# A convolution and an MLP on one core: W_out and block 2's x move to GpSimd's DMA ring, the tap diagonals move to VectorE

## The chip, the cores and the metric

The kernel runs on one core of one Trainium2 chip. The metric is the device time of one execution in microseconds. It was measured in 13 runs before the change: median 686.0, lowest 682.02, highest 687.27. The profile is that of a single execution. It has its own time (685.98) and a span from the first to the last instruction (684.2), which is 1.74 us shorter.

The engines are called as in the profile: PE is TensorE (PEld its weight loads), DVE is VectorE, ACT is ScalarE, POOL is GpSimd, SP is SyncE. SP and ACT issue DMAs into hardware queues (q1 and q10 in the profile), POOL into a software queue (q0).

## What is computed

The input x has 8 sequences of 4096 tokens and 192 channels. Each channel is filtered by a causal convolution of 7 taps, whose weights are a softmax over the taps, one set for each group of 24 channels. Then follows an MLP on 32768 tokens: 192 to 2048 channels, exact gelu, 2048 back to 192.

```python
w = np.exp(w - max); w = w / (sum + 1e-9)                 # weight: 8 heads x 7 taps
out[b, s, h, g] = sum_k w[h, k] * x_pad[b, s + k, h, g]   # 6 zeros ahead of each sequence
h = x @ w_in                                              # 192 -> 2048
g = 0.5 * h * (1 + erf(h / sqrt(2)))
y = g @ w_out                                             # 2048 -> 192, f32
```

Inputs and output are f32.

## The kernel before

**Tiling.** The tokens are split in two halves of 16384, which stand on partitions 0 to 63 and 64 to 127; 192 channels make three column pieces p of 64. The halves are cut into blocks n: six of 256 tokens per half, then blocks of 512 (`WS`). For each block the first product (`mm1`, line 740) runs in units: 8 of them for a block of 256 tokens, each with 12 matmuls and two 128-wide pieces of the 2048 channels. One gelu on ACT (line 652, 128x1024) empties a unit. PE alternates between two PSUM tiles for it (`hp`), so unit u waits for the gelu of unit u - 2. The second product of block n - 1 (`mm2`, line 771, for the small blocks, `mm2_t`, line 801, later) is spread behind the units of block n: 128 matmuls behind 8 units. The list `share` says how many come behind which unit of block 1; without an entry every unit gets the same, 16 matmuls.

**Convolution.** For blocks 0 and 1 (`PC`) PE does it with diagonal matrices: `dg` holds 7 diagonals of 64x64, made from the identity `idb` and the softmax weights `wcol` (line 397, on POOL). Each tap is a pair of matmuls (`pconv`, line 682). The bf16 copy of x that they read comes from transposes of `xin` on DVE (`trans`, line 508), then a cast by ACT for block 0 (line 225) and by POOL for block 1 (line 227). The sums leave PSUM by ACT and DVE (`conv_out`, lines 200 and 202). Block 0's taps come first of all; block 1's stand behind block 0's units 3, 4 and 5 (`behind`). From block 2 on DVE convolves: one transpose, then a first tap (line 529, or ACT's line 625 for blocks 4 to 6) and six more (line 536), and `mm1` of the block waits for the last.

**Loads.** Every DMA is issued in the order in which its engine's program stands. SP: the small weight, half of block 0's x, then a wait until W_in's second part has landed (`S_WIN[1]`), three chunks of W_out in f32 (line 853), block 2's x, the fourth chunk, block 3's x, and from there block n + 3 and the stores of block n - 1 in turn. ACT: the other half of block 0's x. POOL: two DMAs of W_in (f32 in HBM, bf16 in SBUF: the transfer casts; line 376), two of block 1's x, the diagonals when the softmax is ready, two more of block 1's x, W_in's second pair, a wait for the diagonals, `halo(1)` (the 6 tokens ahead of block 1, line 421), the three casts of block 1, `halo(2)`, and then for each chunk of W_out a wait for its landing and a cast to bf16 (line 431), which PE's second product waits for (`S_WOG`, line 838). W_in is loaded for one half of the channels on each partition half; DVE copies it across (`dup`, line 472).

**Warm-up.** PE starts with 10 matmuls of 512 columns on a zeroed tile (`warm`, line 666), behind DVE's memset of that tile.

Of the kernel before, what the change touches and what calls it, by code (L numbers as in the profile page):

```python
# [5 lines left out]
ALU = mybir.AluOpType  # L6
# [5 lines left out]
def bass_lightweight_conv__then__act_gelu_exact_kernel(  # L12
# [83 lines left out]
    def sbt(name, shape, dt):  # L96
        return es.enter_context(nc.sbuf_tensor(name, shape, dt))
# [4 lines left out]
    def sem(name):  # L102
        return es.enter_context(nc.semaphore(name))

    def ap(t, off, pat):
        return bass.AP(t, off, pat)

    with es:
# [7 lines left out]
        wnt = sbt("wnt", [32, 32], F32)  # L116
        wex = sbt("wex", [H, KS], F32)
        wcol = sbt("wcol", [128, 32], F32)
        woutf = sbt("woutf", [128, NF * C], F32)
        idb = sbt("idb", [128, 64], BF16)  # L120
        dg = sbt("dg", [128, KS * 64], BF16)
        warm = sbt("warm", [128, 512], BF16)
        hot = sbt("hot", [1, 2], F32)
        xTb = [sbt("xTb%d" % i, [128, NP * XB], BF16) for i in range(len(PC))]
        xin = [sbt("xin%d" % i, [128, TB // 32 * DQ], F32) for i in range(NX)]
# [8 lines left out]
        S_WSB = sem("S_WSB")  # L134
        S_WIN = [sem("S_WIN%d" % i) for i in range(3)]
        S_WOUT = [sem("S_WOUT%d" % i) for i in range(4)]
        S_WOG = sem("S_WOG")
        S_XIN = [sem("S_XIN%d" % i) for i in range(NX)]
        S_XP = sem("S_XP")
        S_OUT = [sem("S_OUT%d" % i) for i in range(2)]  # L140
        S_MSET = sem("S_MSET")
        S_IDN = sem("S_IDN")
        S_WARM = sem("S_WARM")
        S_PRO = sem("S_PRO")
        S_ACTP = sem("S_ACTP")
        S_DG = sem("S_DG")
# [73 lines left out]
        def cast(e, n, p):  # L220
            e.wait_ge(S_TR, NP * n + p + 1)
            dst = ap(xTb[PC[n]], p * XB + HX, [[NP * XB, 128], [1, WS[n]]])
            src = ap(xT[n % 2], p * XW + HX, [[NP * XW, 128], [1, WS[n]]])
            if n == 0:
                ins = e.activation(out=dst, in_=src, func=AF.Copy)  # L225
            else:
                ins = e.tensor_copy(dst, src)
            ins.then_inc(S_CAST[PC[n]])
# [13 lines left out]

        def xin_at(n):

            return 64 * (n // NX + (n % NX != 1))

        def banks(m, g):

# [123 lines left out]
        @block.gpsimd  # L372
        def _(g):
            def win_in(c0, c1, sm):
                for hf in range(2):
                    g.dma_start(
                        ap(win, 64 * hf * NP * F + c0, [[NP * F, 64], [F, NP], [1, c1 - c0]]),
                        ap(wint, hf * FH + c0, [[NP * F, 64], [F, NP], [1, c1 - c0]]),
                    ).then_inc(sm[hf], 16)
# [13 lines left out]
            win_in(FP[0], FP[1], [S_WIN[0]] * 2)  # L393
            load(g, 1, (0, 2), S_XP)
            g.wait_ge(S_PRO, 9)
            g.wait_ge(S_IDN, 2)
            g.tensor_tensor(  # L397
                ap(dg, 0, [[KS * 64, 128], [64, KS], [1, 64]]),
                ap(idb, 0, [[64, 128], [0, KS], [1, 64]]),
                ap(wcol, 0, [[32, 128], [1, KS], [0, 64]]),  # L400
                ALU.mult,
            ).then_inc(S_DG)
            load(g, 1, (1, 3), S_XP)
            win_in(FP[1], FP[2], S_WIN[1:])

            g.wait_ge(S_DG, 1)

            def halo(n):

                t, tw = (xTb[PC[n]], XB) if n in PC else (xT[n % 2], XW)  # L410
                dst = ap(t, HF, [[NP * tw, 128], [tw, NP], [1, HB]])
                if n >= 4:
                    g.wait_ge(S_CV, cvd(n - 2))
                if OFF[n] % SEQ == 0:
# [6 lines left out]
                g.tensor_copy(dst, src).then_inc(S_HALO)  # L421

            g.wait_ge(S_IDN, 2)
            halo(1)
            for p in range(NP):
                cast(g, 1, p)
            halo(2)
            for k in range(4):
                g.wait_ge(S_WOUT[k], 16)
                pat = [[NF * C, 128], [8 * C, 2], [1, 2 * C]]  # L430
                g.tensor_copy(ap(wout, 2 * k * C, pat), ap(woutf, 2 * k * C, pat)).then_inc(S_WOG)  # L431
            for n in range(3, NB):
                halo(n)

        @block.vector
        def _(v):
            v.memset(warm[:, :], 0.0).then_inc(S_WARM)  # L437
            v.memset(idb[:, :], 1.0).then_inc(S_MSET)
            v.memset(wnm[:, :], 0.0).then_inc(S_MSET)
            v.memset(ap(xTb[0], HF, [[NP * XB, 128], [XB, NP], [1, HB]]), 0.0).then_inc(S_HALO)  # L440
# [44 lines left out]
            def trans(n, p):  # L485

                w = WS[n]
                if p == 0:
                    v.wait_ge(S_XP if n == 1 else S_XIN[n % NX], 64 if n == 1 else xin_at(n))
                    if n >= 2 and n - 2 in PC:  # L490
                        wait_pc(v, n - 2, NP - 1)
                    elif n >= 2:
                        v.wait_ge(S_CV, cvd(n - 2))
                    if n >= 2:
                        v.wait_ge(S_HALO, n)
                if n in PC:
# [11 lines left out]
                v.transpose(out, src).then_inc(S_TR)  # L508
# [45 lines left out]
                else:  # L554
                    conv(*op[1:])

            for p in range(NP):
                trans(0, p)
            for j in PV:
                conv_out(v, 0, j)  # L560
# [100 lines left out]

        @block.tensor
        def _(t):
            t.wait_ge(S_WARM, 1)
            for i in range(10):
                t.matmul(hp[1][:, 0:512], warm[:, 0:128], warm[:, :])  # L666

            def pconv(n, kd, k):

# [26 lines left out]
            for kd in [0] * 4 + [1, 0] * 3 + [1, 2, 2] * 3 + [1, 2] + [3] * 7:  # L696
                pconv(*seq[kd].pop(0))

            behind = {
                (0, 3): [(1, kd, k) for k in taps if k > 3 for kd in (0, 1)],  # L700
                (0, 4): [(1, kd, k) for k in taps if k <= 3 for kd in (0, 1)],
                (0, 5): [(1, kd, k) for k in taps for kd in (2, 3)],
            }

            def mm1(n, i):
                w, c = WS[n], NCH[n]
# [73 lines left out]
                    ins.then_inc(S_MM2 if ph == 1 else S_PH)  # L780


            share = {1: [4, 4, 4, 10, 10, 10, 11, 11]}

            def mm2_t(m, ps, i):

# [39 lines left out]
            for n in range(NB):  # L826
                todo = units(n - 1) if n >= 1 else []
                for i in range(NSL[n]):
                    mm1(n, i)
                    for q in behind.get((n, i), []):  # L830
                        pconv(*q)
                    new = M0 < n <= M1
                    ws = SHARE if new else share.get(n, [1] * NSL[n])
                    a0 = len(todo) * sum(ws[:i]) // sum(ws)
                    a1 = len(todo) * sum(ws[: i + 1]) // sum(ws)
                    for un in todo[a0:a1]:
                        if n == 1 and un[:2] == (0, 0) and un[2] % 4 == 0:
                            t.wait_ge(S_WOG, 1 + un[2] // 4)
                        (mm2_t if new else mm2)(n - 1, *un)
            m = NB - 1  # L840
            for g2 in range(0, NG[m], 2):
# [5 lines left out]
        @block.sync  # L847
        def _(sp):
            sp.dma_start(wsb[:, :], ap(wt, 0, [[KS, H], [1, KS]])).then_inc(S_WSB, 16)
            load(sp, 0, (0, 1))  # L850

            def wout_in(k):
                sp.dma_start(  # L853
                    ap(woutf, 2 * k * C, [[NF * C, 128], [8 * C, 2], [1, 2 * C]]),
                    ap(woutt, 256 * k * C, [[2 * C, 128], [1024 * C, 2], [1, 2 * C]]),
                ).then_inc(S_WOUT[k], 16)

            sp.wait_ge(S_WIN[1], 16)
            for k in range(3):
                wout_in(k)  # L860
            load(sp, 2)
            wout_in(3)
            load(sp, 3)
            for n in range(1, NB):
                if n + 3 < NB:
                    load(sp, n + 3)
                store(sp, n - 1)
            for g in range(NG[NB - 1]):
# [31 lines left out]
```

## Time and profile before

| what | value |
|---|---|
| median of 13 runs | 686.0 us (682.02 to 687.27) |
| profiled execution | 685.98 us, span 684.2 us, mean granted clock 0.998 |
| PE busy | 676.3 us, 99% of the span |
| ACT, DVE, POOL busy | 536.5, 528.2, 31.9 us (78%, 77%, 5%) |
| chain that ended last | 96% PE, 2% DMA, 1% SP's queue |
| W_out's chunks, issue by SP | 11.19 to 12.8 (three), 15.38 (the fourth) |
| POOL's casts of the chunks begin | 14.68, 16.80, 18.99, 22.47 us |

A line of the timeline has the start in us, the length of the group in us, engine, line of the kernel, operation, output and inputs, shape and count; in square brackets is how long the engine stood idle before it and what ended that. The chain is the work that ended last, followed back from the end. A row of stretches gives the length, the busy time of PE, PEld, DVE, ACT and POOL with the number of instructions in brackets, the granted clock of PE (1.00 is full), the share of the DMA engines and GB/s.

### The profile page before, as it was taken

The numbers are of one execution on the slowest core, as the hardware profiler recorded it, in microseconds if no ns is written. First come the engines' busy times: TensorE is split into PE (matmuls) and PEld (weight loads), VectorE is DVE, ScalarE is ACT, GpSimd is POOL, SyncE is SP. The second block draws the span as 40 slices with busy tenths as digits, with TensorE's granted clock in tenths as the row PEclk, the third lists the DMA queues.
The fourth block names the chain that finished last, engine by engine and source line by source line (L and its number), as shares of the span: only waits on it lengthen the run. The fifth ranks groups of instructions, "written<-read, shape, count | busy, mean of one in ns | idle before, by whom it ended". The sixth has DMA issues, their size and how long they took to land.

```text
span 684.2 us, 26995 instructions
## 1 busy us (share of the span) xinstructions
PE 676.3 (99%) x12570; PEld 409.0 (60%) x12570; DVE 528.2 (77%) x610; ACT 536.5 (78%) x547; POOL 31.9 (5%) x56
## 2 busy tenths in 40 slices
PE   8899999999999999999999999999999999999998
PEld 5799755555555555555555555555555555555557
DVE  6779989777798777798777897777897777987511
ACT  7699987777787877778777778777877777877772
POOL 5100000000000000000000000000000000000000
PEclk9999999999999999999999999999999999999999
DMA  7544421244432244422334322334322434220123
GB/s 167 102 117 106 95 71 48 50 94 95 94 84 45 62 94 95 94 71 44 77 94 95 93 58 47 87 94 95 90 50 52 95 94 94 71 54 21 48 49 94
DMA packets 132480, 54.43 MB, mean 80 GB/s; under 512 B 126352, under 2 KB 132304, under 8 KB 132368
## 3 DMA queue, kind: packets, MB, share of 16 engines
q1 hardware_dynamic: 130224, 50.94, 31.8%
q8 instruction: 98, 1.61, 1.1%
q0 software_dynamic: 1024, 1.18, 1.0%
q10 hardware_dynamic: 1120, 0.59, 0.3%
q14 instruction: 14, 0.11, 0.1%
HBM read 28.31 MB, written 25.17 MB: 78 GB/s over the span
## 4 chain that ended last, share of the span: by engine, by line
PE 96%; DMA 2%; SPq 1%; POOL 0%; DVE 0%; issue 0%; ACT 0%; ACTq 0%
PE hp L740 47%; PE ob L801 42%; PE ob L771 6%; DMA woutf<-in_moe_w_out_dram 1%; PE hp L771 1%; DMA win<-in_moe_w_in_dram 1%; SPq L853 0%; SPq L339 0%; DMA wsb<-in_weight_dram 0%; POOL xin L339 0%; POOL wout L431 0%; POOL dg L397 0%; DVE wcol L460 0%; ACT wex L593 0%; DVE osb L295 0%
## 5 line engine op out<-in xcount | busy, mean ns | idle before, releaser
L652 ACT ACTIVATE gT<-hp 128x1024 bf16<-128x1024 f32 x512 | 523.1, 1024 | 133.3 <-PE hp L740 130.0
L740 PE MATMUL hp<-xc,win 64*64 64x512 bf16 (+2 forms) x6048 | 419.1, 366 | 1.1 <-ACT gT L652 0.9
L801 PE MATMUL ob<-gT,wout 64*64 64x512 bf16 x5376 | 366.3, 376 | 0.0
L536 DVE SCALAR_TENSOR_TENSOR acc<-xT,wcol,acc 128x1024 f32<-128x1024 f32 (+1 forms) x330 | 296.1, 946 | 5.3 <-ACT acc L625 5.3
L740 PEld LDWEIGHTS hp<-xc,win 64*64 64x64 bf16 (+1 forms) x6048 | 188.2, 106 | 135.4 <-ACT gT L652 2.2
L801 PEld LDWEIGHTS ob<-gT,wout 64*64 64x64 bf16 x5376 | 172.3, 118 | 122.7
L326 DVE STREAM_TRANSPOSE osb<-ob 128x512 f32<-128x512 f32 x84 | 74.5, 890 | 128.8 <-PE ob L801 128.8
L508 DVE STREAM_TRANSPOSE xT<-xin 128x1536 f32<-128x1536 f32 (+2 forms) x39 | 74.8, 1925 | 4.7 <-DMA xin<-in_x_dram 4.6
L536 DVE SCALAR_TENSOR_TENSOR xc<-xT,wcol,acc 128x1024 bf16<-128x1024 f32 (+1 forms) x66 | 60.6, 958 | 0.0
L771 PE MATMUL ob<-wout,gT 64*128 64x192 bf16 x896 | 48.2, 246 | 2.7 <-POOL wout L431 2.4
L771 PEld LDWEIGHTS ob<-wout,gT 64*128 64x128 bf16 x896 | 39.1, 95 | 8.9 <-POOL wout L431 3.1
L421 POOL COPY xT<-xT 128x18 f32<-128x18 f32 x30 | 20.0, 667 | 511.2 <-DVE xT L508 483.0
L529 DVE TENSOR_SCALAR acc<-xT,wcol 128x512 f32<-128x512 f32 (+2 forms) x60 | 33.7, 604 | 1.1
L297 ACT ACTIVATE osb<-ob 128x192 f32<-128x192 f32 x2 | 0.7, 331 | 7.1 <-PE ob L771 7.1
L771 PE MATMUL hp<-wout,gT 64*128 64x192 bf16 x128 | 5.9, 243 | 0.0
L666 PE MATMUL hp<-warm 128*128 128x512 bf16 x10 | 4.4, 632 | 1.3 <-DVE warm L437 1.3
L295 DVE COPY osb<-ob 128x192 f32<-128x192 f32 x2 | 0.7, 357 | 6.1 <-PE ob L771 6.1
L771 PEld LDWEIGHTS hp<-wout,gT 64*128 64x128 bf16 x128 | 5.3, 94 | 0.0
L625 ACT ACTIVATE acc<-xT,wcol 128x256 f32<-128x256 f32 (+1 forms) x9 | 5.2, 575 | 0.0
L202 DVE CAST xc<-ob 64x256 bf16<-64x256 f32 (+3 forms) x8 | 2.9, 357 | 3.0 <-PE ob L682 2.8
L282 ACT ACTIVATE osb<-ob 128x384 f32<-128x384 f32 x10 | 4.9, 486 | 0.0
L682 PEld LDWEIGHTS ob<-xTb,dg 64*64 64x64 bf16 x112 | 3.3, 118 | 1.6 <-ACT xTb L225 0.9
(36 smaller groups left out, 30.9 us busy)
## 6 DMA issues: line engine op xcount, KB each, us to landing
out_dram<-osb SPq DMA_DIRECT2D x124, 192.0 KB, 3.1
xin<-in_x_dram SPq DMA_DIRECT2D x116, 192.0 KB, 4.1
xin<-in_x_dram SPq DMA_DIRECT2D x18, 96.0 KB, 4.6
woutf<-in_moe_w_out_dram SPq DMA_DIRECT2D x4, 384.0 KB, 5.6
win<-in_moe_w_in_dram POOLq DMA_DIRECT2D x4, 192.0 KB, 4.7
xin<-in_x_dram POOLq DMA_DIRECT2D x4, 96.0 KB, 3.4
out_dram<-osb ACTq DMA_DIRECT2D x4, 96.0 KB, 1.9
out_dram<-osb SPq DMA_DIRECT2D x4, 96.0 KB, 2.6
```

Of the source, the lines that this page charges most:

```text
L282: e.activation(out=dst, in_=src, func=AF.Copy).then_inc(S_EVA)
L326: v.transpose(ap(osb[m % 2], j, [[8 * C, 128], [C // 2, TB // 32], [NP, 32]]), bank(ring(m, j)),).then_inc(S_EV)
L421: g.tensor_copy(dst, src).then_inc(S_HALO)
L508: v.transpose(out, src).then_inc(S_TR)
L529: ins = v.tensor_scalar(a, src, wk, None, ALU.mult)
L536: ins = v.scalar_tensor_tensor(dst, src, wk, a, op0=ALU.mult, op1=ALU.add)
L625: a.activation(out=acc[n % 2][:, p * TB : p * TB + w], in_=ap(xT[n % 2], p * XW + HX, [[NP * XW, 128], [1, w]]), func=AF.Copy, scale=wcol[ ...
L652: a.activation(out=ap(gT[n % 2], i * c * 2 * w, dst), in_=ap(hp[u % 2], 0, src), func=AF.Gelu,).then_inc(S_GELU)
L666: t.matmul(hp[1][:, 0:512], warm[:, 0:128], warm[:, :])
L740: ins = t.matmul(hp[u % 2][fo : fo + fw, o : o + w], ap(win, f1, [[NP * F, 64], [2, fw]]), xc[n % 2][r, p * TB : p * TB + w], start=(p == ...
L771: ins = t.matmul(bb[sub], gT[m % 2][r, c0 : c0 + 128], wout[r, CH[sub][i] * C : (CH[sub][i] + 1) * C], start=(ph == 0 and k == 0), stop=(p ...
L801: ins = t.matmul(bank(ring(m, j), slice(64 * h, 64 * h + 64), w), ap(wout, 64 * hf * NF * C + CH[h][i] * C + j, [[NF * C, 64], [NP, 64]],) ...
```

## The change

W_out is now loaded by four DMAs that POOL issues and that cast to bf16 on the way; they stand behind W_in and `halo(1)` and ahead of block 1's casts. POOL's casts of W_out, the f32 buffer and its semaphore are gone; PE waits for the DMAs themselves. Block 2's x is issued by POOL too, behind block 1's casts and ahead of `halo(2)`, with a semaphore of its own. SP waits for it before it loads block 3. The diagonals are made by DVE, between the first and the second transpose of block 0, and POOL no longer waits for the softmax. The four DMAs of block 1's x stand together ahead of W_in's second pair. `share` is empty, so the second product of block 0 is spread evenly behind the units of block 1. Block 1's taps are spread over units 3 to 6 of block 0. The warm-up has 11 matmuls on a constant that is there from the start; the memset of `warm` is gone. `xin_at` counts the loads of the `xin` buffers anew, as block 2 no longer uses the common semaphore.

```diff
@@ POOL
             win_in(FP[0], FP[1], [S_WIN[0]] * 2)
-            load(g, 1, (0, 2), S_XP)
-            g.wait_ge(S_PRO, 9)
-            g.wait_ge(S_IDN, 2)
-            g.tensor_tensor(
-                ap(dg, 0, [[KS * 64, 128], [64, KS], [1, 64]]),
...
-            ).then_inc(S_DG)
-            load(g, 1, (1, 3), S_XP)
+            load(g, 1, sm=S_XP[0])
             win_in(FP[1], FP[2], S_WIN[1:])
-
-            g.wait_ge(S_DG, 1)
...
             halo(1)
+            for k in range(4):
+                g.dma_start(
+                    ap(wout, 2 * k * C, [[NF * C, 128], [8 * C, 2], [1, 2 * C]]),
+                    ap(woutt, 256 * k * C, [[2 * C, 128], [1024 * C, 2], [1, 2 * C]]),
+                ).then_inc(S_WOUT[k], 16)
             for p in range(NP):
                 cast(g, 1, p)
+            load(g, 2, sm=S_XP[1])
             halo(2)
-            for k in range(4):
-                g.wait_ge(S_WOUT[k], 16)
-                pat = [[NF * C, 128], [8 * C, 2], [1, 2 * C]]
-                g.tensor_copy(ap(wout, 2 * k * C, pat), ap(woutf, 2 * k * C, pat)).then_inc(S_WOG)
@@ DVE
-            v.memset(warm[:, :], 0.0).then_inc(S_WARM)
             v.memset(idb[:, :], 1.0).then_inc(S_MSET)
...
-                    v.wait_ge(S_XP if n == 1 else S_XIN[n % NX], 64 if n == 1 else xin_at(n))
+                    v.wait_ge(S_XP[n - 1] if n in (1, 2) else S_XIN[n % NX], 64 if n in (1, 2) else xin_at(n))
...
-            for p in range(NP):
+            trans(0, 0)
+            v.wait_ge(S_PRO, 9)
+            v.wait_ge(S_IDN, 2)
+            v.tensor_tensor(
+                ap(dg, 0, [[KS * 64, 128], [64, KS], [1, 64]]),
+                ap(idb, 0, [[64, 128], [0, KS], [1, 64]]),
+                ap(wcol, 0, [[32, 128], [1, KS], [0, 64]]),
+                ALU.mult,
+            ).then_inc(S_DG)
+            for p in range(1, NP):
                 trans(0, p)
@@ PE
-            t.wait_ge(S_WARM, 1)
-            for i in range(10):
-                t.matmul(hp[1][:, 0:512], warm[:, 0:128], warm[:, :])
+            one = nc.const_aps.tensor(1.0, (128, 512), BF16)
+            for i in range(11):
+                t.matmul(hp[1][:, 0:512], one[:, 0:128], one)
...
-            behind = {
-                (0, 3): [(1, kd, k) for k in taps if k > 3 for kd in (0, 1)],
-                (0, 4): [(1, kd, k) for k in taps if k <= 3 for kd in (0, 1)],
-                (0, 5): [(1, kd, k) for k in taps for kd in (2, 3)],
-            }
+            p01 = [(1, kd, k) for k in taps for kd in (0, 1)]
+            p2 = [(1, kd, k) for k in taps for kd in (2, 3)]
+            behind = {(0, 3): p01[:6], (0, 4): p01[6:12], (0, 5): p01[12:] + p2[:6], (0, 6): p2[6:]}
...
-            share = {1: [4, 4, 4, 10, 10, 10, 11, 11]}
+            share = {}
...
-                            t.wait_ge(S_WOG, 1 + un[2] // 4)
+                            t.wait_ge(S_WOUT[un[2] // 4], 16)
@@ SP
-            sp.wait_ge(S_WIN[1], 16)
-            for k in range(3):
-                wout_in(k)
-            load(sp, 2)
-            wout_in(3)
+            sp.wait_ge(S_XP[1], 64)
             load(sp, 3)
```

More of the change, by code (lines that the diff above doesn't have):

```diff
@@ L118, in bass_lightweight_conv__then__act_gelu_exact_kernel @@
         wcol = sbt("wcol", [128, 32], F32)
-        woutf = sbt("woutf", [128, NF * C], F32)
         idb = sbt("idb", [128, 64], BF16)
         dg = sbt("dg", [128, KS * 64], BF16)
-        warm = sbt("warm", [128, 512], BF16)
         hot = sbt("hot", [1, 2], F32)
@@ L136, in bass_lightweight_conv__then__act_gelu_exact_kernel @@
         S_WOUT = [sem("S_WOUT%d" % i) for i in range(4)]
-        S_WOG = sem("S_WOG")
         S_XIN = [sem("S_XIN%d" % i) for i in range(NX)]
-        S_XP = sem("S_XP")
+        S_XP = [sem("S_XP%d" % i) for i in range(2)]
         S_OUT = [sem("S_OUT%d" % i) for i in range(2)]
@@ L142, in bass_lightweight_conv__then__act_gelu_exact_kernel @@
         S_IDN = sem("S_IDN")
-        S_WARM = sem("S_WARM")
         S_PRO = sem("S_PRO")
@@ L243, in xin_at @@
         def xin_at(n):
-            return 64 * (n // NX + (n % NX != 1))
+            return 64 * (n // NX + (n % NX == 0))
         def banks(m, g):
@@ L393, in _ @@
             win_in(FP[0], FP[1], [S_WIN[0]] * 2)
-            load(g, 1, (0, 2), S_XP)
-            g.wait_ge(S_PRO, 9)
-            g.wait_ge(S_IDN, 2)
-            g.tensor_tensor(
-                ap(dg, 0, [[KS * 64, 128], [64, KS], [1, 64]]),
-                ap(idb, 0, [[64, 128], [0, KS], [1, 64]]),
-                ap(wcol, 0, [[32, 128], [1, KS], [0, 64]]),
-                ALU.mult,
-            ).then_inc(S_DG)
-            load(g, 1, (1, 3), S_XP)
+            load(g, 1, sm=S_XP[0])
             win_in(FP[1], FP[2], S_WIN[1:])
-            g.wait_ge(S_DG, 1)
             def halo(n):
@@ L850, in _ @@
             load(sp, 0, (0, 1))
[L852 to L856, printed above, removed]
-            sp.wait_ge(S_WIN[1], 16)
-            for k in range(3):
-                wout_in(k)
-            load(sp, 2)
-            wout_in(3)
+            sp.wait_ge(S_XP[1], 64)
             load(sp, 3)
```

## The prediction

> **What bounds the kernel now.** I read the shares first: PE is busy 99% of the span and the chain that ended last is 96% PE, so nothing that runs beside PE after the start is worth anything. Next I read the chain over the first 30 us, where it is not PE:
>
> ```profile
> 6.74 4.44 DMA win<-in_moe_w_in_dram
> ...
> 13.38 0.47 SPq L339
> ...
> 15.38 7.04 DMA woutf<-in_moe_w_out_dram
> 22.47 0.95 POOL wout L431
> ```
>
> W_in's second half lands at 11.18, only then SP issues W_out's chunks; the fourth stands behind block 2's x, lands at 22.42 and is cast on POOL until 23.41. The timeline of PE shows what that does (start, duration, group, idle before it):
>
> ```profile
> 16.96 0.83 PE L740 MATMUL hp<-xc,win 64*128 64x256 bf16 x12 [0.45 <-ACT gT L652]
> ...
> 23.47 1.51 PE L771 MATMUL ob<-wout,gT 64*128 64x192 bf16 x20 [2.43 <-POOL wout L431]
> ...
> 32.52 0.82 PE L740 MATMUL hp<-xc,win 64*128 64x256 bf16 x12
> 33.18 0.82 PE L771 MATMUL ob<-wout,gT 64*128 64x192 bf16 x16
> 33.84 0.82 PE L740 MATMUL hp<-xc,win 64*128 64x256 bf16 x12
> ...
> 43.05 0.82 PE L740 MATMUL hp<-xc,win 64*128 64x256 bf16 x12
> ```
>
> Block 1's first unit starts at 16.96, block 2's at 32.52: 15.56 us for eight units. Block 2, with the same matmuls (12 of L740 and 16 of L771 a unit), takes 43.05 - 32.52 = 10.53 us. So block 1 loses 5.0 us. The stretches say how (PE busy, then PEld, DVE, ACT, POOL, granted clock, DMA share, GB/s):
>
> ```profile
> 20.87:24.29 3.42, 0.92 (x18) 0.54 (x16) 3.38 (x6) 1.02 (x1) 1.53 (x2) 1.00 1.05 177
> 24.29:27.70 3.41, 3.41 (x45) 2.98 (x42) 3.41 (x8) 1.02 (x1) 0.00 (x0) 0.50 0.03 7
> ```
>
> PE has 0.92 us of work in the first, and in the next 3.41 us it is granted half its clock, about 1.7 us lost on top of the waiting.
>
> Last, what else could hold block 2:
>
> ```profile
> 20.73 1.21 DVE L508 STREAM_TRANSPOSE xT<-xin 128x768 f32<-128x768 f32 x1 [4.60 <-DMA xin<-in_x_dram]
> ...
> 28.50 1.14 DVE L536 SCALAR_TENSOR_TENSOR xc<-xT,wcol,acc 128x512 bf16<-128x512 f32 x2
> ```
>
> x of block 2 lands at 20.7; its convolution ends at 28.50 + 1.14 = 29.64. That is hidden today (PE comes at 32.52), but would bound block 2 as soon as more than 2.9 us were saved. So the 5.0 us need both transfers earlier.
>
> **The change part by part.**
>
> *The software ring.* What it carries is in one row of the queues:
>
> ```profile
> q0 software_dynamic: 1024, 1.18, 1.0%
> ```
>
> 1.18 MB (W_in, 4 x 192 KB, cast, and block 1's x, 4 x 96 KB) took 1.0% of 16 engines' span, 6.8 us (6.5 to 7.2 by rounding). The change puts the same volumes behind it: W_out cast is 4 x 192 KB, block 2's x 4 x 96 KB. So another 6.8 us, of which W_out is two thirds, 4.5.
>
> *POOL's order of issue.* The diagonals (0.94) leave POOL between x's second and third issue, with the 0.2 us wait before them; a DVE memset of 0.27 no longer stands ahead of the memset POOL waits for.
>
> ```profile
> 5.56 1.18 POOL L339 DMA_DIRECT2D xin<-in_x_dram  x2
> 6.74 1.24 POOL L376 DMA_DIRECT2D win<-in_moe_w_in_dram  x2
> 7.97 0.21 POOL L421 CAST xTb<-xT 128x18 bf16<-128x18 f32 x1
> 10.60 1.48 POOL L227 CAST xTb<-xT 128x256 bf16<-128x256 f32 x3 [2.41 <-DVE xT L508]
> ```
>
> W_in's second pair is issued at about 5.7 instead of 6.74 and lands at about 10.2 instead of 11.18. Block 1's halo, then W_out's four issues, 4 x 0.63 (the W_in row's 1.24 for two) = 2.5 us, run from 7.2 to 9.7, inside the idle 2.41 us ahead of the cast L227. If that cover is gone, everything over it delays the cast one for one. Block 2's x, 4 x 0.6 = 2.4, follows the casts, 12.4 to 14.8; queued behind it is only block 2's halo (0.2), wanted after block 2's transpose, and the fifth and later halos, idle today.
>
> *Landings.* W_out behind W_in: 10.2 + 4.5 = 14.7 for the fourth chunk, block 2's x 2.3 later, about 17.0; I take 15.5 and 17.8, allowing 0.8 for receipt. Low end: the Trainium skill, "DMA: Bandwidth & Descriptors", section "Anatomy of one DMA", prices a software DMA at 2.0 us plus bytes over 436 GB/s; 1.57 MB of f32 read then needs 3.6 us, W_out there at 13.8. High end: the pace of the hardware chunks today, one per 2.15 us (POOL got them at 14.68, 16.80, 18.99) after 3.4 for the first: from 10.2 that is 13.6 to 20.1, and x at 22.4. The q0 row is nearest: same queue, same kind of cast. With an even share PE wants chunks 0 and 1 at 17.7, 2 and 3 at 19.0 to 19.5: all late ends but the last are harmless. SP's loads of blocks 3 and 4 wait for block 2's x: issued 17.8 to 21.8, as now (15.88 to 21.80); wanted from 25.7.
>
> *What goes.* Four POOL casts (0.83 to 0.94) and SP's W_out issues leave; W_out waits on PE become DMA waits. One DVE instruction that took 1.31 beside the last cast should take 0.74.
>
> *Diagonals on DVE.* 128x448, two sources. No such DVE row; nearest is L536's 128x512 at 0.74 and 128x256 at 0.47, so 0.67, start to start 0.6. Ends: 0.35 (as L529's one-source 256) and 0.94 (POOL's own). They start after the first transpose (4.62 + 0.45) and are ready at 5.74 against 5.62 today. Queued behind: block 0's second and third transposes, ACT's casts of them, PE's taps of piece 1: each 0.6 later. PE has four taps of piece 0 to cover part; I put the first L740 0.3 us later (8.6), ends 0.1 and 0.6.
>
> *Taps of block 1* go from 12, 16 and 28 matmuls behind units 3, 4, 5 to 12, 12, 16, 16 behind 3 to 6. ACT bounds this stretch (gelus of 1.02 back to back, three gaps of 0.19, 0.30, 0.26). One more switch, about 0.2, falls behind unit 6; units 4 and 5 get 0.1 each shorter. Unit 6's gelu, which lets block 1 start, comes at 15.95 instead of 15.88: the 0.3 is nearly absorbed. Block 1's last copies out of PSUM end at about 17.2, wanted at 17.5. Ends for the start of block 1: 16.7 and 17.6; I take 17.0.
>
> *Warm-up* of 11 instead of 10 matmuls starts 0.4 earlier, 11 x 0.43 = 4.7, done before the diagonals: nothing.
>
> *Sum.* Block 2 starts at 17.0 + 10.53 = 27.5 instead of 32.52. Its convolution: 17.8 + (28.50 + 0.74 - 20.73) - 0.57 = 25.7 for the first two thirds, 26.2 for all, hidden by 1.8 us. Block 3's: 17.7 us later than x (20.73 to 39.03 now), 35.6, against PE at 38.0. From block 4 on DVE waits for ACT's first taps (L625), which go by PE's pace and move with it. So 5.0 us reach the end: span 684.2 - 5.0 = 679.2; the profiled execution, 685.98 at 684.2, gives **681.0**, and as the median of the 13 runs is 686.0, the same for it.
>
> **Rules weighed.** The granted clock fell after a wait of 2.43 us in a stretch that held 0.92 us of matmul. The Trainium skill, "TensorE: Matmul & The Clock Gate", section "HAM oscillation", says gaps over about 3.4 us throttle: by it today's wait would be free of that loss and the gain 5.0 - 1.7 = 3.3 if the wait goes; the row shows 0.50, so 5.0. Against the change speaks "SBUF — State Buffer", section "Who interferes with whom": a VectorE copy in a two-port mode locks GpSimd out, which then cannot write descriptors. Row: L472's two copies, 0.69 each, at 8.58 (8.9 after) fall into W_out's issues; a POOL cast beside a later one took 0.65 instead of 0.40. By the rule W_out's issue ends at 9.7 + 1.4 = 11.1, the casts start 0.2 to 0.3 late, and block 2's x is late by another 1.4: 19.2, convolution 27.1. Still hidden. By the row, 0.25 each. I take the row.
>
> **Rivals.**
> (A) Both transfers in time: 681.0.
> (B) The ring is slower than W_in's row, and block 2's convolution takes over. It decides from x later than 19.5 (27.5 - 7.95). For: everything now stands in one queue, x last. Against: that queue moved the same volume in 6.8 us. At x = 20.7, as today: 20.7 + 7.95 = 28.65, gain 3.9, 682.1; at 22.4: 30.35, gain 2.2, 683.8.
> (C) The clock is released one stretch of 3.41 us later, since DVE's diagonals open a hole of up to 0.6 us in PE's warm-up: up to 1.7 lost, 682.7. Against: today's warm-up is followed by a small hole too.
> (D) Slower: W_out's four issues hold POOL, so block 1's casts L227, PE's taps in order behind unit 3 and all after come late. Gain is eaten when the casts start 5 us late, at about 15.9, that is with (15.9 - 7.2) / 4 = 2.2 us an issue instead of 0.63 (a ring that fills and makes POOL wait for W_in to drain). At 3 us an issue the casts start at 19.2, 8.3 late: 689.3. Against: eight issues in a row went at 0.58 to 0.82.
> (E) It does not do what it says: the fourth chunk still comes at about 22.4. Then only the POOL cast's 0.95 goes: 685.0.
>
> **How the numbers follow.** A 0.66, B 0.17, C 0.08, E 0.04, D 0.05. Range 679.5 (diagonals, tap spread and clock release at their good ends, 1.5 better) to 683.8 (B's late end): holds A, B and C. About 0.2% (1.4 us) is what a measurement of this kernel can tell from no change; A, B and C are faster (0.91), E within (0.04), D slower (0.05).
>
> **What would show it.** PE without a wait on W_out, clock 1.00 from 8 us on; block 2's first unit near 27.5 and then 10.5 a block; W_out's fourth landing by 16.5, block 2's transpose before 18.5; the casts L227 within 0.5 of 10.9. Wrong: DVE still waiting for x past 19.5, POOL issues over 1 us, a PE wait in front of block 1's taps.

## The result and the profile after

The change makes the kernel faster. Its median is 680.85 us (680.73 to 681.45, 11 runs), beside 685.53 (682.02 to 687.5, 48 runs) for the kernel before on the same chip; the ratio is 0.9938, with a 95% interval of 0.9924 to 0.9953. The profiled execution took 680.89 us with a span of 679.1: 5.1 less than before on both counts. One further run stood at 683.63 with a mean granted clock of 0.997 and is not among the 11 (with it the median would be 680.87), while the runs of before with such a clock are counted; such runs are taken up below.

The lines of the kernel have moved: `mm1` is L733 (was L740), `mm2` L764 (L771), the taps L677 (L682), POOL's casts L223 (L227), the transposes L494 (L508), the convolution on DVE L522 (L536).

First the chain of waits (start, length, what), in excerpts; behind 16.78 only PE follows:

```profile
1.64 3.22 DMA xin<-in_x_dram
...
6.85 1.02 PE ob L677 x28
...
9.24 1.95 ACT gT L647 x2
...
16.78 0.95 PE hp L733 x12
17.73 0.66 PE ob L764 x16
```

The pieces for W_in, the issue on SP behind it, W_out and POOL's cast (4.44 + 0.47 + 7.04 + 0.95 = 12.9 us of it before) are gone. What is left ahead of block 1 is block 0's x, the diagonals on DVE, the taps, and the gelus. Block 1's first unit begins at 16.78. Next PE's timeline:

```profile
12.00 0.52 PE L677 MATMUL ob<-xTb,dg 64*64 64x256 bf16 x12
...
15.94 1.79 PE L733 MATMUL hp<-xc,win 64*128 64x256 bf16 x24
17.57 0.82 PE L764 MATMUL ob<-wout,gT 64*128 64x192 bf16 x16
...
27.44 0.82 PE L733 MATMUL hp<-xc,win 64*128 64x256 bf16 x12
...
37.96 0.82 PE L733 MATMUL hp<-xc,win 64*128 64x256 bf16 x12
```

No group of block 1 shows an idle time in brackets: W_out is never waited for. Block 2 starts at 27.44 instead of 32.52, 5.08 us earlier. Block 1 takes 27.44 - 16.78 = 10.66 us, block 2 takes 37.96 - 27.44 = 10.52. The two stretches that showed the loss now read:

```profile
20.87:24.29 3.42, 3.42 (x76) 3.21 (x74) 3.42 (x8) 2.61 (x3) 0.00 (x0) 1.00 0.67 161
24.29:27.70 3.41, 3.41 (x80) 3.24 (x76) 3.41 (x7) 3.06 (x4) 0.00 (x0) 1.00 0.20 61
```

PE is busy throughout (before: 0.92 us in the first) and has its full clock in the second (before: 0.50). POOL's timeline, the landing times of W_out as the trace sums them up, and the queue's row:

```profile
5.27 1.25 POOL L372 DMA_DIRECT2D win<-in_moe_w_in_dram  x2
...
10.68 1.47 POOL L223 CAST xTb<-xT 128x256 bf16<-128x256 f32 x3 [0.43 <-DVE xT L494]
12.10 2.39 POOL L335 DMA_DIRECT2D xin<-in_x_dram  x4
```

```profile
L411 POOL DMA_DIRECT2D wout<-in_moe_w_out_dram x4: 716/718/751, 7.4 to 9.5; - x4
...
DMA to landing us min/median/max: 6.3/7.0/7.8
```

```profile
q0 software_dynamic: 2304, 2.36, 2.1%
```

W_out's four issues take 0.72 each and still fit ahead of the casts, with 0.43 us to spare. The last is issued at 9.5 and takes the longest, so it lands at 9.5 + 7.8 = 17.3. The ring now carries 2.36 MB in 2.1% of the span, 14.3 us: twice the volume for about twice the time. On DVE:

```profile
18.45 1.22 DVE L494 STREAM_TRANSPOSE xT<-xin 128x768 f32<-128x768 f32 x1 [1.38 <-DMA xin<-in_x_dram]
...
25.69 1.14 DVE L522 SCALAR_TENSOR_TENSOR xc<-xT,wcol,acc 128x512 bf16<-128x512 f32 x2
```

Block 2's x lands at 18.4, and its convolution ends at 25.69 + 1.14 = 26.83, 0.6 us before PE wants it.

### The profile page after: what moved, and what is told of

The parts are those of the page before. It is cut to its first block, busy times and chain, and to the rows that moved or that the text cites. A ratio compares the mean times of both kernels' runs of the same rounds, so it can differ in the third digit from the quotient of the medians.

```text
span 679.1 us, 26993 instructions
## 1 busy us (share of the span) xinstructions
PE 673.4 (99%) x12571; PEld 408.7 (60%) x12571; DVE 527.4 (78%) x610; ACT 536.5 (79%) x547; POOL 35.4 (5%) x59
## 3 DMA queue, kind: packets, MB, share of 16 engines
q0 software_dynamic: 2304, 2.36, 2.1%
## 4 chain that ended last, share of the span: by engine, by line
PE 98%; DMA 0%; ACT 0%; DVE 0%; issue 0%; SPq 0%
PE hp L733 49%; PE ob L794 43%; PE ob L764 5%; PE hp L764 1%; DMA xin<-in_x_dram 0%; PE ob L677 0%; ACT gT L647 0%; DVE dg L546 0%; DVE xT L494 0%; ACT xTb L221 0%; SPq L842 0%; ACT xc L196 0%; DVE osb L291 0%; SPq L335 0%
## 5 line engine op out<-in xcount | busy, mean ns | idle before, releaser
L733 PE MATMUL hp<-xc,win 64*64 64x512 bf16 (+2 forms) x6048 | 418.6, 366 | 0.7 <-ACT gT L647 0.5
L522 DVE SCALAR_TENSOR_TENSOR acc<-xT,wcol,acc 128x1024 f32<-128x1024 f32 (+1 forms) x330 | 295.5, 947 | 3.2 <-ACT acc L620 3.2
L733 PEld LDWEIGHTS hp<-xc,win 64*64 64x64 bf16 (+1 forms) x6048 | 188.1, 106 | 134.3 <-ACT gT L647 1.7
L494 DVE STREAM_TRANSPOSE xT<-xin 128x1536 f32<-128x1536 f32 (+2 forms) x39 | 74.6, 1920 | 1.6 <-DMA xin<-in_x_dram 1.5
L522 DVE SCALAR_TENSOR_TENSOR xc<-xT,wcol,acc 128x1024 bf16<-128x1024 f32 (+1 forms) x66 | 60.4, 953 | 0.0
L406 POOL COPY xT<-xT 128x18 f32<-128x18 f32 x30 | 22.6, 752 | 512.2 <-DVE xT L494 489.2
L764 PE MATMUL ob<-wout,gT 64*128 64x192 bf16 x896 | 46.8, 243 | 0.0
L764 PEld LDWEIGHTS ob<-wout,gT 64*128 64x128 bf16 x896 | 38.6, 94 | 5.1 <-issue 0.4
L764 PE MATMUL hp<-wout,gT 64*128 64x192 bf16 x128 | 5.9, 243 | 0.0
L764 PEld LDWEIGHTS hp<-wout,gT 64*128 64x128 bf16 x128 | 5.3, 94 | 0.0
L677 PE MATMUL ob<-xTb,dg 64*64 64x256 bf16 (+1 forms) x112 | 3.9, 248 | 1.4 <-ACT xTb L221 1.4
L661 PE MATMUL hp<-const-bfloat16-1.0 128*128 128x512 bf16 x11 | 4.0, 538 | 0.8 <-PEq L868 0.8
```

The source lines that it names most:

```text
L522: ins = v.scalar_tensor_tensor(dst, src, wk, a, op0=ALU.mult, op1=ALU.add)
L661: t.matmul(hp[1][:, 0:512], one[:, 0:128], one)
L733: ins = t.matmul(hp[u % 2][fo : fo + fw, o : o + w], ap(win, f1, [[NP * F, 64], [2, fw]]), xc[n % 2][r, p * TB : p * TB + w], start=(p == ...
L764: ins = t.matmul(bb[sub], gT[m % 2][r, c0 : c0 + 128], wout[r, CH[sub][i] * C : (CH[sub][i] + 1) * C], start=(ph == 0 and k == 0), stop=(p ...
```

## The experiments

Names that begin with b are the kernel before with one thing altered, those with a the changed kernel. Each group ran on one chip together with the kernel before; a ratio is against those runs. The mean granted clock of each run is recorded too, and it turned out to matter: over the three groups the kernel before ran 79 times, 35 times at a clock of 1.000 (median 683.64) and 44 times at 0.994 to 0.999 (median 686.01).

### b_fill: keep PE busy in the wait for W_out's last chunk

```diff
+    if un[2] == 12:
+        for _ in range(10):
+            t.matmul(bank(3), warm[:, 0:128], warm[:, :])
     t.wait_ge(S_WOG, 1 + un[2] // 4)
```

> The kernel before, with ten matmuls of 512 columns on the zeroed tile ahead of PE's wait for W_out's fourth chunk; they write a bank that nobody uses at that time. Theory: of the 5 us that block 1 loses, about 1.7 are the halved clock after the wait, so with PE kept busy the clock stays at 1.00 from 24 to 28 us, block 2 starts 1.7 earlier (near 30.8) and the time falls from about 685.5 to about 683.9, with the runs closer together. Rival (the clock has no part of its own, the wait costs all): the time stays at 685.5, or rises by up to 0.3 where the ten matmuls outlast the wait.

684.0 us (683.53 to 684.78, 12 runs), ratio 0.9985 (0.9972 to 0.9998). PE's timeline of the profiled run (684.78, span 683.0):

```profile
20.92 2.33 PE L840 MATMUL ob<-warm 128*128 128x512 bf16 x10
23.95 1.24 PE L771 MATMUL ob<-wout,gT 64*128 64x192 bf16 x20 [0.70 <-POOL wout L431]
```

The wait is as long as ever: the second product goes on at 23.95, even 0.48 later than before, because POOL's cast took 1.34 us in this run instead of 0.94. Yet the span is 1.2 us shorter. The clock stayed at 1.00, so the halved stretch was worth 1.2 + 0.48 = 1.7 us, as read from the row of before. (From that group to block 2's first unit it is 31.35 - 23.95 = 7.40 us, beside 32.52 - 23.47 = 9.05 before.) All 12 runs were at 1.000 and lie within 1.25 us of each other. So the wait costs in two ways, its own length and, in part of the runs, the clock behind it.

### b_ring: W_out in the ring, and nothing else

```diff
@@ POOL, behind halo(1)
+    for k in range(4):
+        g.dma_start(
+            ap(wout, 2 * k * C, [[NF * C, 128], [8 * C, 2], [1, 2 * C]]),
...
+        ).then_inc(S_WOUT[k], 16)
     for p in range(NP):
         cast(g, 1, p)
     halo(2)
-    for k in range(4):
-        g.wait_ge(S_WOUT[k], 16)
...
@@ SP
...
-    for k in range(3):
-        wout_in(k)
     load(sp, 2)
-    wout_in(3)
@@ PE
-    t.wait_ge(S_WOG, 1 + un[2] // 4)
+    t.wait_ge(S_WOUT[un[2] // 4], 16)
```

Block 2's x stays with SP, the diagonals with POOL, and the old spreads remain.

> The kernel before with one part of the change alone: W_out by the casting DMAs on POOL behind W_in, PE waits for them; block 2's x stays with SP behind W_in's second half, diagonals on POOL, taps and the share of the second product as before. Theory (W_out's way to PE is the whole gain): no wait on W_out, clock 1.00, time 681.0 to 681.9 (block 1's casts start about 0.5 later, as POOL's issues end near 11.2). Rival (block 2's x or the diagonals carry a part): over 682.5, with DVE or PE waiting elsewhere.

681.72 us (681.28 to 682.34, 8 runs), ratio 0.9954 (0.9937 to 0.997); profiled span 679.9, 4.3 less than before. PE's timeline:

```profile
17.20 0.83 PE L741 MATMUL hp<-xc,win 64*128 64x256 bf16 x12 [0.45 <-ACT gT L653]
...
28.21 0.82 PE L741 MATMUL hp<-xc,win 64*128 64x256 bf16 x12
```

Block 2 starts 4.31 us earlier than before; that is 85% of the whole change. The other 0.77 is in two places: the changed kernel starts block 1 at 16.78 instead of 17.20 (0.42), and takes 10.66 instead of 11.01 for it (0.35). The step does three things at once, which no run separates: W_out is issued earlier (from 8.13 on, instead of 11.19 to 15.38), POOL's cast goes, and block 2's x on SP no longer stands behind three chunks. Nor was it tried whether SP would do as well. Before the change it issued nothing from 2.1 to 11.19, because of its wait for W_in; W_out ahead of that wait, or the fourth chunk ahead of block 2's x, remains open.

### a_share, a_behind, a_dgpool, a_x2sp: take back one of the small parts

Each takes back one part; in a_dgpool DVE's instruction for the diagonals goes as well.

```diff
@@ a_share
-            share = {}
+            share = {1: [4, 4, 4, 10, 10, 10, 11, 11]}
@@ a_behind
...
-            behind = {(0, 3): p01[:6], (0, 4): p01[6:12], (0, 5): p01[12:] + p2[:6], (0, 6): p2[6:]}
+            behind = {
+                (0, 3): [(1, kd, k) for k in taps if k > 3 for kd in (0, 1)],
+                (0, 4): [(1, kd, k) for k in taps if k <= 3 for kd in (0, 1)],
+                (0, 5): [(1, kd, k) for k in taps for kd in (2, 3)],
+            }
@@ a_dgpool, POOL
-            load(g, 1, sm=S_XP[0])
+            load(g, 1, (0, 2), S_XP[0])
+            g.wait_ge(S_PRO, 9)
+            g.wait_ge(S_IDN, 2)
+            g.tensor_tensor(
...
+            ).then_inc(S_DG)
+            load(g, 1, (1, 3), S_XP[0])
             win_in(FP[1], FP[2], S_WIN[1:])
+            g.wait_ge(S_DG, 1)
@@ a_x2sp, POOL
-            load(g, 2, sm=S_XP[1])
@@ a_x2sp, SP
-            sp.wait_ge(S_XP[1], 64)
+            sp.wait_ge(S_WIN[1], 16)
+            load(sp, 2, sm=S_XP[1])
             load(sp, 3)
```

> The changed kernel with the old list of shares (4, 4, 4, 10, 10, 10, 11, 11) behind block 1's units. Theory: the even share does not shorten PE's work, it only had to wait until W_out is early; the light first units are then ACT's (gelu 1.02 against 0.98 of PE), and block 1 takes up to 0.5 longer, as in the kernel with W_out alone on the ring (11.0 instead of 10.5 between the first units of blocks 1 and 2): 681.1 to 681.4. Rival (the share carries a good part of the gain): 682 or more.

> The changed kernel with block 1's taps as before, 12, 16 and 28 matmuls behind units 3, 4 and 5. Theory by the prediction's sum: 0.1 later to 0.1 earlier, 680.75 to 680.95. Rival (the spread is what made block 1's first unit come at 16.78, 0.2 earlier than the prediction said): 681.0 to 681.2.

> The changed kernel with the diagonals on POOL again, between the second and third DMA of block 1's x. Theory: W_in's second half, W_out's issues and block 1's casts come 0.5 to 1.0 later; PE waits about 0.3 for W_in at unit 4, block 2's x lands near 19 and its convolution just keeps up: 680.9 to 681.3. Rival (moving the diagonals is worth as much as W_out, or is harmful by DVE's 0.6 in front of block 0's transposes): 682 or more, or below 680.6.

> The changed kernel with block 2's x on SP, issued when W_in's second half has landed, beside W_out on POOL's ring. Theory: the same bytes; x lands earlier (15 to 17), W_out's fourth chunk later than 17.3 but before 19.2, when PE wants it: 680.7 to 681.0. Rival (two queues at once slow W_out past 19.2): PE waits on W_out again, 681.5 or more, with halved clock in some runs.

| kernel | median, runs | ratio (95%) | runs at clock 1.000 |
|---|---|---|---|
| a_share | 681.55 (681.26 to 684.4), 8 | 0.9941 (0.9919 to 0.9964) | 7: 681.26 to 682.18 |
| a_behind | 682.18 (680.84 to 683.71), 12 | 0.9957 (0.9939 to 0.9974) | 8: 680.84 to 682.3 |
| a_dgpool | 681.43 (680.86 to 682.95), 9 | 0.9942 (0.9924 to 0.996) | 6: 680.86 to 681.44 |
| a_x2sp | 682.19 (680.78 to 684.31), 12 | 0.9959 (0.994 to 0.9977) | 6: 680.78 to 682.64 |

The medians of a_behind and a_x2sp are raised by runs with a lower clock (4 and 6 of 12), and some of their runs at full clock stand up to 1.5 and 1.9 us above their fastest, which no trace explains; so the traces are the better witness. With the old `share` block 1 takes 30.93 - 19.79 = 11.14 us instead of 10.66, 0.5 longer, which agrees with its fastest run (681.26 against 680.73). In a_behind the time from block 0's third unit to block 1's first is 19.49 - 12.80 = 6.69 us against 16.78 - 10.32 = 6.46: the new spread of the taps is worth 0.2. The diagonals on POOL delay everything behind them in its program: W_in's second pair is issued at 7.00 instead of 5.27, W_out from 8.67 instead of 7.35, and block 1's casts begin at 11.50 instead of 10.68. (0.29 us of it is that the softmax began later in this run, at 2.45 instead of 2.16.) PE pays for the late casts. The chain of waits, then PE's timeline:

```profile
8.71 2.87 POOL wout L422 x4
11.58 0.85 POOL xTb L223 x2
12.43 0.04 issue
12.48 0.52 PE ob L680 x10
```

```profile
12.13 0.86 PE L680 MATMUL ob<-xTb,dg 64*64 64x256 bf16 x12 [0.45 <-POOL xTb L223]
...
27.99 0.82 PE L736 MATMUL hp<-xc,win 64*128 64x256 bf16 x12
```

PE does not wait for W_in's second pair there, as had been expected, but for the casts: it is rival D's step on a small scale. Block 2 comes 0.55 later than 27.44, and the profiled time, 681.44, is 0.55 above 680.89; the medians of the runs at full clock differ by 0.4 (681.2 and 680.85). So this part of the change gains about half a microsecond through the order of POOL's work, not by faster diagonals. With block 2's x on SP, the transpose at 19.41 follows the last copy out of PSUM without a wait, in a run whose block 0 had begun 2 us late, and the fastest run is 680.78. Once W_out is off SP's queue, no cost of loading block 2's x on SP was found; but half of a_x2sp's runs had the lower clock, against 2 of 19 of the changed kernel itself, and it is not shown whether its edit has a part in that.

### a_x2late: rival B's step alone

```diff
     for p in range(NP):
         cast(g, 1, p)
+    for k in range(3):
+        g.memset(scr[:, 1024 * k : 1024 * k + 1024], 0.0)
     load(g, 2, sm=S_XP[1])
```

`scr` is a tile that nothing reads.

> The changed kernel with the same three memsets behind block 1's casts, ahead of the issue of block 2's x, which lands that much later than 18.4. Theory (case B's threshold): block 2's convolution then ends 0.6 to 0.7 us of slack behind, so a delay of 2.5 costs about 1.8 to 1.9 at block 2, but blocks 3 to 5 have slack and keep the loss, 682.7. Rival (the loss is caught up by later blocks, as DVE has idle time): below 681.5.

683.48 us (680.96 to 684.51, 12 runs), ratio 0.998 (0.9963 to 0.9996); the profiled run 681.93, 0.8 below the theory's 682.7. Its timelines of DVE and of PE:

```profile
20.25 1.23 DVE L497 STREAM_TRANSPOSE xT<-xin 128x768 f32<-128x768 f32 x1 [3.34 <-DMA xin<-in_x_dram]
```

```profile
28.38 0.92 PE L736 MATMUL hp<-xc,win 64*128 64x256 bf16 x12 [0.93 <-DVE xc L525]
```

x of block 2 lands only 1.8 us later instead of 2.5, and block 2 starts 0.94 later, which is the extra wait. The profiled time rises by 1.04, so the later blocks do not catch it up. Block 2 comes 28.38 - 20.25 = 8.13 after x. So B decides once x lands later than 27.44 - 8.13 = 19.3, and the changed kernel has 0.9 left: the 0.6 from the end of the convolution to PE, and 0.25 because `mm1` starts before it needs the last piece. Its median stands higher than its trace: five runs have a lower clock (684.24 to 684.51), but three at full clock stand at 683.28 to 683.49, and no trace shows what held those.

### a_poolcast: hold back block 1's casts with memsets

The same three memsets ahead of the casts instead of behind them.

> The changed kernel with three memsets of 128x1024 on POOL between W_out's issues and block 1's casts, some 2.5 us by estimate, to spend the cover that the prediction's case D is about. Theory: only 0.4 us of cover is left there, so PE's taps behind unit 3 and all after come later by the memsets' length less 0.4: about 683.0 for 2.5. Rival (the casts have slack, as ACT bounds this stretch and not PE's taps): less than half of that, under 682.0.

686.54 us (685.28 to 688.96, 12 runs), ratio 1.0034 (1.0016 to 1.0053): slower than the kernel before, though the casts were held only until 14.00. The timelines of POOL, of DVE and of PE say why:

```profile
10.09 2.75 POOL L417 MEMSET scr<- 128x1024 f32 x3
```

```profile
8.48 4.90 DVE L461 COPY win<-win 64x1536 bf16<-64x1536 bf16 x2
```

```profile
10.09 3.29 DVE L461 COPY win<-win 64x1536 bf16<-64x1536 bf16 x1
```

```profile
13.53 1.70 PE L736 MATMUL hp<-xc,win 64*128 64x256 bf16 x24 [3.81 <-DVE win L461]
```

The two copies of W_in on DVE took 4.90 us instead of 1.42. The second (the third of these lines is that copy alone) began with the memsets and outlasted all three: 3.29 us instead of 0.7. PE waited for that, not for the casts, and the clock was halved behind the wait. The experiment shows that POOL can hold DVE, and not what it was made for.

### a_wait0: hold back block 1's casts with a wait

```diff
+    g.wait_ge(S_WOUT[0], 16)
     for p in range(NP):
         cast(g, 1, p)
```

> Rival D's step by itself, without use of the SBUF port: POOL waits for W_out's first chunk (landed at 13.65) before it casts block 1's pieces, so the casts start at 13.7 instead of 10.7. D's own arithmetic (all but the idle time ahead of the cast goes to the end one for one): first taps of block 1 at 14.6 instead of 12.0, block 2's first unit at 29.9 to 30.1 instead of 27.4, 683.3 to 683.6, and up to 1.7 more in runs where the wait of 2.5 us halves the clock. If ACT's gelus, not the taps, bound this stretch, less than half of it arrives: 681.0 to 682.2, first unit of block 2 before 28.7.

682.95 us (682.35 to 684.87, 12 runs), ratio 0.9969 (0.9953 to 0.9985); its control a_again stood at 680.82. POOL and PE of the profiled run (682.84):

```profile
13.16 1.09 POOL L223 CAST xTb<-xT 128x256 bf16<-128x256 f32 x3 [3.02 <-DMA wout<-in_moe_w_out_dram]
```

```profile
13.61 0.86 PE L678 MATMUL ob<-xTb,dg 64*64 64x256 bf16 x12 [1.58 <-POOL xTb L223]
...
29.38 0.82 PE L734 MATMUL hp<-xc,win 64*128 64x256 bf16 x12
```

The casts start 2.48 us later than at 10.68, block 2 starts 1.94 later than at 27.44, and the time is 682.84 - 680.89 = 1.95 higher. D's arithmetic is nearly right: block 1's taps do stand on the path. Of the missing 0.54, 0.38 is the casts' own length, as they ran without DVE's copies beside them (1.09 instead of 1.47); I take the rest to be that the taps had not been late before, which is not shown. Gelus on ACT don't hide the delay.

### a_again, a_lag, a_warm16: the runs with a lower clock

In the profiled runs of a_share, a_behind and a_x2sp block 0's x arrived at 6.2 to 6.7 us, so that PE stood after its warm-up; in the other traces the transposes of it start at 4.6 to 4.9. a_again is the changed kernel unaltered; `lag` is a tile of 128x512 bf16 that nothing reads.

```diff
@@ a_lag, DVE
+            v.memset(lag[:, :], 0.0)
             v.memset(idb[:, :], 1.0).then_inc(S_MSET)
@@ a_warm16, PE
-            for i in range(11):
+            for i in range(16):
```

> The changed kernel once more, as the control for the next two: in three profiled runs of its variants block 0's x landed at 6.2 to 6.6 us instead of 4.9, PE stood 1.9 to 2.9 us after its warm-up, and the clock was halved in the stretch that followed. If that is an accident of the start and not of those variants, some of this kernel's runs show it too: runs at clock 1.000 at 680.7 to 681.5, the others at clock 0.997 to 0.998 and 682.8 to 684.5, median between 680.9 and 683. If the variants caused it, all runs stand at 680.7 to 681.5 and clock 1.000.

> The memset of the old warm-up operand put back on VectorE ahead of the diagonal's memset, so that the software ring's first transfer is issued 0.27 us later, as in the kernel before. If the earlier issue makes block 0's x late in part of the runs, its runs all stand at clock 1.000 and 680.9 to 681.8 while the control shows some at 0.997. If the earlier issue has no part in it, it has as many runs at 0.997 as the control.

> 16 instead of 11 warm-up matmuls, which end at about 5.9 instead of 4.9, just ahead of the first taps at 6.06. If it is PE's hole after the warm-up that halves the clock, a late x of block 0 costs 1.0 us less hole (about 1.1 instead of 2.2) and the clock stays: all runs at 1.000, 680.8 to 682.3, the higher ones those with x late. If the hole's length doesn't decide, as many runs at 0.997 and 683 to 684 as the control.

| kernel | median, runs | ratio (95%) | runs below clock 1.000 |
|---|---|---|---|
| a_again | 680.82 (680.73 to 682.68), 7 | 0.9939 (0.9918 to 0.996) | 1 |
| a_lag | 680.71 (680.61 to 681.37), 6 | 0.9936 (0.9913 to 0.9959) | 0 |
| a_warm16 | 682.09 (680.74 to 682.59), 9 | 0.9946 (0.9928 to 0.9964) | 0 |

The control shows such a run (682.68 at 0.997), so the changed kernel has them too. a_lag, which starts the ring 0.28 us later (1.83 instead of 1.55), as before, has none in 6 runs; one in seven against none in six separates nothing. Over all groups the evidence is larger: of the kernels without an added wait, those with the later start (b_fill, b_ring, a_lag) had none in 26 runs, those with the earlier start (the changed kernel, a_again, a_share, a_behind, a_x2sp) 13 in 51, six of them in a_x2sp (left out are a_dgpool, with 3 in 9, and a_warm16). In the profiled runs DVE never waits for block 0's x with the later start (four traces, the kernel before among them); with the earlier start it does in four traces of ten, by 0.17 us in the changed kernel's and by 1.5 to 2.0 in those three. That would fit a ring whose first transfers delay block 0's x, but no run shows it: these kernels differ in other things and ran in different groups. The cause stays open. 16 warm-up matmuls kept the clock in all 9 runs, yet seven of them lie above 681.5; no trace shows what those waited for, and it is no gain. Neither is measurably faster than the change.

## Why the prediction was right

**What bounded the kernel: right, in both its parts.** The loss of 5.0 us in block 1 was nearly all regained: block 1 takes 10.66 instead of 15.56, which is 4.90, and starts 0.18 earlier, 5.08 together. b_fill separates the 1.7 us of the clock; b_ring shows that W_out alone brings 4.31.

**The ring: the sum stands, its start and its order were wrong.** The q0 row gave 6.8 us for the second half of the ring; the row after gives 14.3 - 6.8 = 7.5, by rounding 6.7 to 8.1, so it does not contradict that. W_out's fourth chunk was put at 15.5, by 16.5, and landed at 17.3. Of the two DMAs of W_in's second pair the prediction took the landing of the first, 10.2 (measured 5.27 + 4.8 = 10.1); W_out stands behind the second as well, which landed at 5.9 + 6.0 = 11.9. From there the prediction's own 4.5 and 0.8 give 17.2. (No run separates this from a share of W_out that is larger than 4.5.) By the same step block 2's x, 2.3 behind W_out, would have come at 19.5, where B begins to decide. But x did not wait for all of W_out. Its first DMA landed at 12.1 + 3.8 = 15.9, ahead of W_out's third (8.8 + 7.5 = 16.3) and fourth, and its last at 18.4, 1.1 behind W_out:

```profile
L372 POOL DMA_DIRECT2D win<-in_moe_w_in_dram x1: 626/626/626, 5.9 to 5.9; - x1
...
DMA to landing us min/median/max: 6.0/6.0/6.0
```

```profile
L335 POOL DMA_DIRECT2D xin<-in_x_dram x1: 659/659/659, 12.1 to 12.1; - x1
...
DMA to landing us min/median/max: 3.8/3.8/3.8
```

(Both of the changed kernel, the DMA chosen by a window.) So the 17.8 for x came near by two errors that offset each other, a start too early and an order too strict, which is luck. The late fourth chunk cost nothing, since PE begins the second product at 17.57 and comes to that chunk only in the group at 18.89. The price of 2.0 us plus bytes, the low end, had given 13.8. Block 2's x, at 18.4 instead of 17.8, used up about half of its slack: the first two thirds of the convolution were to be hidden by 1.8 us and end at 25.69 + 0.74 = 26.43, hidden by 1.0; all of it by 1.3, and is hidden by 0.6. The margin to B shrank from 1.7 us (17.8 against 19.5) to 0.9 (18.4 against 19.3).

**POOL's order: right.** W_in's second pair at 5.27 (5.7 predicted), casts at 10.68 (10.9), x's issues 12.10 to 14.49 (12.4 to 14.8); W_out's issues took 0.72 each, not 0.63. a_dgpool shows that this order is worth about half a microsecond, through the start of block 1's casts; the prediction had not put that down as a gain of its own.

**Diagonals on DVE, taps, start of block 1: right, a little pessimistic.** The diagonals took 0.58 instead of 0.67 and PE's first unit came at 8.37 instead of 8.6. Block 1 started at 16.78 (17.0), block 2 at 27.44 (27.5).

**The rivals.** B and D were right in their arithmetic (8.13 us from x to block 2 instead of 7.95; 1.94 us for 2.48 of delay) and wrong in their premise, for B that the ring, for D that POOL's issues are slow enough. E fell: no wait on W_out is left. C's mechanism, a hole behind the warm-up that halves the clock, does occur in part of the runs, but from a late x of block 0; and as the diagonals now stand behind that x's transpose, they are late with it:

```profile
7.41 0.63 PE L677 MATMUL ob<-xTb,dg 64*64 64x256 bf16 x8 [1.87 <-DVE dg L546]
```

(a_behind, PE's timeline.) With the full clock on both sides the change still does better: 680.85 against 683.64.

**A step that was lucky.** The profiled execution of before was taken to stand for its median because both were 686.0. It had the halved stretch, as 44 of the 79 runs of the groups did. Had only 4 runs of 10 drawn it, the median before would have stood near the upper end of the others, at some 684.5 (an estimate), and a gain of 5.0 read from one trace would have been over 1 us too large. The forecast of the time after was not touched by this, as that trace has its own sum. Against all 48 runs the gain is 685.53 - 680.85 = 4.7 us.

**The rules weighed.** By the 3.4 us rule of the Trainium skill, "TensorE: Matmul & The Clock Gate", section "HAM oscillation", the gain was 3.3; by the row, 5.0. The runs of before at full clock give 683.64 - 680.85 = 2.8 us, the others 686.01 - 680.85 = 5.2. So neither is the whole answer; but the wait of 2.43 us, which the rule would let pass, did halve the clock. The two groups of before lie 2.4 apart, 0.7 more than a halved stretch is worth; what the rest is, no trace shows. Of the skill's page "SBUF — State Buffer", section "Who interferes with whom": VectorE's copies did not hold POOL's DMA issues as the rule would have it. The issue ahead of the copies (7.35 to 8.10) took 0.75, those beside them 0.72, so neither the rule's 1.4 nor the row's 0.25 for each copy is seen. But POOL memsets did hold a VectorE copy.

## What to carry to other kernels

Look for the wait that ends last in the start-up and issue what it waits for from a queue that does not itself stand in a wait; here moving four DMAs from behind SP's wait into the ring gave 4.3 of 5.1 us. Price a PE wait twice, for its length and for the clock that may be halved behind it, and look at the clock of many runs before one trace is taken for the median. When a queue is loaded further, follow the item that now stands last in it, here block 2's x, and write down how much slack it has left. Count from the landing of the last DMA ahead of it, not of the first.

## What the hardware showed that was not expected

**The clock goes by fixed stretches, not by the length of a wait.** The granted clock changes only on a grid of 3.41 us, whose position differs from run to run. Rows of stretches on that grid (PE busy is the first number behind the comma, the granted clock the third from the end), for a_share, a_behind and a_poolcast:

```profile
5.43:8.84 3.41, 1.04 (x17) 0.60 (x20) 1.86 (x4) 1.10 (x3) 1.24 (x3) 1.00 1.05 208
8.84:12.26 3.42, 3.42 (x64) 2.79 (x58) 1.77 (x4) 1.18 (x5) 2.91 (x5) 0.50 0.98 138
```

```profile
5.24:8.66 3.42, 1.39 (x27) 0.80 (x28) 1.86 (x4) 1.24 (x3) 1.46 (x4) 1.00 1.09 216
8.66:12.07 3.41, 3.41 (x58) 2.70 (x54) 2.10 (x4) 1.38 (x4) 2.89 (x4) 0.50 1.03 144
```

```profile
7.85:11.26 3.41, 1.72 (x34) 1.30 (x28) 3.32 (x4) 2.44 (x4) 3.41 (x6) 1.00 1.16 148
11.26:14.68 3.42, 1.16 (x22) 1.19 (x24) 3.39 (x4) 0.28 (x1) 2.23 (x4) 1.00 1.14 172
14.68:18.09 3.41, 3.41 (x43) 1.53 (x38) 1.46 (x3) 2.30 (x3) 3.33 (x7) 0.50 0.33 77
```

A stretch with 0.92 (before), 1.04, 1.16 or 1.39 us of PE's work was followed by one at half clock; after 1.72 the clock stayed. In a_x2sp's trace it was 1.16, and no trace of this case that records the clock has a stretch between 1.39 and 1.72 us. The Trainium skill, "TensorE: Matmul & The Clock Gate", section "What's actually happening", says that the window of 3.4 us runs free of the kernel's start, which these rows agree with. It would explain why a wait of some 2.4 us costs the clock in some runs and not in others. With the bound between 1.39 and 1.72, the wait must take 1.69 to 2.02 us out of one stretch, and that is so for 53% to 72% of the positions of the grid (an estimate: (3.41 - 2.43 + 2 x (2.43 - 2.02)) / 3.41 and the same with 1.69). 44 of the 79 runs of before, 56%, had the lower clock, which fits.

**POOL memsets can hold up a bf16 copy on DVE.** In a_poolcast the copy that began with them took 3.29 us instead of 0.7, over three memsets of together 2.75. In a_x2late the same memsets held a copy for one of them only: it began at 12.03, during the first memset (11.94 to 12.89), took 1.40 and ended at 13.43, and the second memset, beside its end, took 1.23 instead of 0.95:

```profile
12.03 1.40 DVE L461 COPY win<-win 64x1536 bf16<-64x1536 bf16 x1
```

```profile
12.83 1.23 POOL L419 MEMSET scr<- 128x1024 f32 x1
```

What decides between the two is open, and so is why the first copy of a_poolcast took 1.58 us (8.48 to 10.06) although it ended before a memset is shown.
